# One core, attention beside an SSM: a rewrite with a played-out order, three-bank exps, tables made once, a bound from |q| and transposed reciprocals

## The chip, the cores and the metric

The kernel runs on one core of a Trainium2 chip. The metric is device microseconds of that core, lower is better.

Engine names as in the profile: PE (TensorE matmuls), PEld (its weight loads), DVE (VectorE), ACT (ScalarE), POOL (GpSimd), SP (the queue that issues most DMAs). A trailing q, as in ACTq, is an engine's instruction sequencer. "Pass" in this document means 512 columns streamed through PE once, by one matmul or by several that run side by side in different parts of the array.

## The reference

Two independent layers, concatenated on the last axis.

```python
# A: a diagonal complex SSM, L = 2048, D = P = 640
dt = exp(log_dt); Lam_bar = exp(dt * Lam)
B_bar = ((Lam_bar - 1) / Lam)[:, None] * Bmat
Bu = einsum("bld,pd->blp", x, B_bar)
h_t = Lam_bar * h_{t-1} + Bu_t                  # 2048 steps
y = 2 * einsum("blp,dp->bld", h, Cmat).real + x * Dskip

# B: attention, 32 query heads of 20, one shared key/value head, S = 2048
q = (x @ wq) in 32 heads; k = x @ wk; v = x @ wv
p = softmax(q k^T * 20**-0.5)                   # 32 x 2048 x 2048
out = (p v, heads joined) @ wo
```

Inputs and output are bf16. The large object is the 134 million softmax weights: 2048 tiles of 128 keys by 512 queries, each of which must go once through ACT's exp.

## The kernel before

Attention is walked in 512 iterations of 4 tiles. Scores need only 21 contraction rows (20 plus one that carries the softmax bound), so four heads sit in PE's four row groups. An iteration scores two tiles into two PSUM banks (SCA), two more into two others (SCB), takes an exp of each pair, and adds the four tiles, multiplied by the values (the PV matmuls), to a PV bank, four column groups at once.

```python
def plan_scores(self, it, half):
    T = self.SCA if half == 0 else self.SCB
    for jj in range(2):
        j = 2 * half + jj
        P.pe(lambda e: e.matmul(T[:, 512*jj:512*jj+512],
             lhsT=P.KT[32*j:32*j+21, 128*kc:128*kc+128],
             rhs=P.QT[32*j:32*j+21, gg, q0:q0+512], tile_position=(32*j, 0), ...), ...)
def plan_exp(self, it, half):                   # 1024 columns each
    P.act(lambda e: e.activation(ptv, T[:, :], ACT.Exp, scale=self.alpha), ...)
def plan_pv(self, it):
    for j in range(4):
        P.pe(lambda e: e.matmul(pvt[32*j:32*j+32, :], lhsT=P.VP[:, kc, 0:32],
             rhs=P.PT[:, buf, j, :], tile_position=(0, 32*j), ...), ...)
```

Everything else is background, laid into these iterations by fixed rates (4 PE steps an iteration, then 3 DVE steps, and so on):

```python
self.BG_PE_PER_IT, self.BG_DVE_PER_IT, self.OUTPROJ_PER_IT = 4, 3, 6
...
def qt_block_ops(self, gg, tb, ps, bkey):
    # q: 5 passes over xbT with wq4; then the bound: 5 more over |x| with wm4 (from |wq| and max|k|)
    ...
def ssm_tables_ops(self, tb):
    # for each of 4 token blocks: 30 DVE steps and 10 Sin activations on ACT
    ...
def norm_tasks(self, gi):
    # sums of 4 heads -> 4 partitions x 512, reciprocal there, broadcast by a matmul
    d2 = ... e.reciprocal(rden, den_ps)         # 4 x 512
```

## Time and profile before

| | before |
|---|---|
| time, median of 4 runs | 1250.8 us (1246.3 to 1251.1) |
| first exp starts, last exp ends, span (timeline) | 73.6, 1226.2, 1249.5 us |
| exps, smallest start-to-start | 1024, 0.903 us |
| mean granted PE clock | 0.705 |

From the page of the kernel before: span, busy time by engine, the slices of PE, ACT and granted clock (in tenths), and the chain of waits.

```profile
span 1249.5 us, 12936 instructions
...
PE 987.0 (79%) x5371; PEld 261.0 (21%) x5442; DVE 513.5 (41%) x772; ACT 1016.6 (81%) x1089; POOL 18.0 (1%) x24
...
PE   2678888887788786888885788888858788889886
...
ACT  4067898989888898888988888898978888898882
...
PEclk9777997986666766776656766766656777675777
...
ACT 51%; PE 36%; DVE 9%; issue 2%; SPq 1%; DMA 0%; ACTq 0%; DVEq 0%
```

ACT and PE are both busy for about 80% of the time and neither is full. The chain passes from one to the other. The clock row holds tenths, but the records behind it know only 0.5 and 1.0; a 7 is a slice that changed in between.

From the page's groups (busy us, mean ns of one, idle before and what ended it), and from the view of waits (us in total, times, longest):

```profile
L780 ACT ACTIVATE PT<-SCA 128x1024 bf16<-128x1024 f32 x512 | 529.6, 1034 | 151.0 <-PE SCB L767 122.1
L780 ACT ACTIVATE PT<-SCB 128x1024 bf16<-128x1024 f32 x512 | 530.6, 1036 | 0.0
...
L817 DVE RECIPROCAL rdenb<-PVB 4x512 bf16<-4x512 f32 x16 | 53.5, 3346 | 37.2 <-PE PVB L812 37.2
```

```profile
ACT PT L780 <- PE SCB L767: 122.1, 90, 2.3
...
ACT PT L780 <- PE SCA L767: 27.3, 53, 4.2
```

ACT waits for scores 143 times for 149 us in all. The timeline shows what such a wait looks like, here at half clock, with background work (line 631) between the score groups:

```profile
320.51 0.62 PE L792 MATMUL PVA<-PT,VP 128*32 128x512 bf16 x4
320.82 1.02 ACT L780 ACTIVATE PT<-SCB 128x1024 bf16<-128x1024 f32 x1
...
321.46 1.49 PE L631 MATMUL M<-xaT,BTre 128*128 128x512 bf16 x3 [0.33 <-issue]
...
322.88 0.61 PE L767 MATMUL SCA<-QT,KT 21*128 21x512 bf16 x2
...
323.55 1.02 ACT L780 ACTIVATE PT<-SCA 128x1024 bf16<-128x1024 f32 x1 [1.72 <-PE SCB L767]
```

Between the exp that starts at 320.82 and the next, at 323.55, PE put background passes before the scores, and ACT stood for 1.72 us. In undisturbed stretches exps start 0.90 to 0.92 us apart.

### The profile page before, as it was taken

How to read it: one execution, taken by the hardware profiler on the slowest of the kernel's cores; microseconds unless marked ns; L12 is line 12 of the kernel's file. 1: busy time of each engine (PE TensorE's matmuls, PEld its weight loads, DVE VectorE, ACT ScalarE, POOL GpSimd, SP SyncE). 2: the span in 40 equal slices, each digit the busy share in tenths (PEclk: the TensorE clock that was granted, in tenths of full speed). 3: DMA queues.
4: the chain of work that ended last, by engine and by line, in shares of the span. 5: the costliest groups of instructions: out<-in, count | busy, mean ns of one | idle time of the engine just before them, and what ended most of it. 6: DMA issues, size and time to landing. Idle time of an engine off the chain costs nothing.

```text
span 1249.5 us, 12936 instructions
## 1 busy us (share of the span) xinstructions
PE 987.0 (79%) x5371; PEld 261.0 (21%) x5442; DVE 513.5 (41%) x772; ACT 1016.6 (81%) x1089; POOL 18.0 (1%) x24
## 2 busy tenths in 40 slices
PE   2678888887788786888885788888858788889886
PEld 1212222221112211221111222211112222111222
DVE  0522211226542278225773242266951213675222
ACT  4067898989888898888988888898978888898882
POOL 5000000000000000000000000000000000000000
PEclk9777997986666766776656766766656777675777
DMA  9700000000000000000000000000000000000000
GB/s 180 142 6 1 1 1 1 1 1 1 1 1 11 11 1 1 11 12 1 1 1 5 17 1 11 11 1 1 1 6 6 17 12 6 1 1 1 11 12 21
DMA packets 44179, 16.29 MB, mean 13 GB/s; under 512 B 38744, under 2 KB 44120, under 8 KB 44120
## 3 DMA queue, kind: packets, MB, share of 16 engines
q1 hardware_dynamic: 44120, 15.46, 5.4%
q8 instruction: 42, 0.69, 0.2%
q14 instruction: 17, 0.14, 0.0%
HBM read 1.69 MB, written 5.24 MB: 6 GB/s over the span
## 4 chain that ended last, share of the span: by engine, by line
ACT 51%; PE 36%; DVE 9%; issue 2%; SPq 1%; DMA 0%; ACTq 0%; DVEq 0%
ACT PT L780 48%; PE SCA L767 5%; PE SCB L767 5%; PE M L631 4%; PE M L516 3%; PE PVA L792 3%; PE PVB L792 3%; PE M L837 3%; PE M L715 2%; DVE rdenb L817 2%; ACT tab L613 2%; PE M L522 1%; PE M L719 1%; PE M L840 1%; SPq L381 1%
## 5 line engine op out<-in xcount | busy, mean ns | idle before, releaser
L780 ACT ACTIVATE PT<-SCA 128x1024 bf16<-128x1024 f32 x512 | 529.6, 1034 | 151.0 <-PE SCB L767 122.1
L780 ACT ACTIVATE PT<-SCB 128x1024 bf16<-128x1024 f32 x512 | 530.6, 1036 | 0.0
L767 PE MATMUL SCB<-QT,KT 21*128 21x512 bf16 x1024 | 262.3, 509 | 118.1 <-ACT PT L780 107.9
L767 PE MATMUL SCA<-QT,KT 21*128 21x512 bf16 x1024 | 267.1, 500 | 74.9 <-ACT PT L780 73.3
L792 PE MATMUL PVA<-PT,VP 128*32 128x512 bf16 x1024 | 134.0, 514 | 0.0
L792 PE MATMUL PVB<-PT,VP 128*32 128x512 bf16 x1024 | 133.7, 511 | 0.3 <-ACT PT L780 0.3
L767 PEld LDWEIGHTS SCA<-QT,KT 21*128 21x128 bf16 x1024 | 50.9, 95 | 288.4 <-ACT PT L780 241.4
L767 PEld LDWEIGHTS SCB<-QT,KT 21*128 21x128 bf16 x1024 | 50.8, 95 | 279.4 <-ACT PT L780 277.2
L526 DVE CAST QT<-M 128x512 bf16<-128x512 f32 x26 | 18.0, 692 | 125.8 <-PE M L522 125.8
L817 DVE RECIPROCAL rdenb<-PVB 4x512 bf16<-4x512 f32 x16 | 53.5, 3346 | 37.2 <-PE PVB L812 37.2
L817 DVE RECIPROCAL rdenb<-PVA 4x512 bf16<-4x512 f32 x16 | 53.5, 3344 | 31.9 <-PE PVA L812 31.8
L742 DVE CAST ystage<-M 128x512 bf16<-128x512 f32 x16 | 11.0, 687 | 115.2 <-PE M L715 115.2
L846 DVE CAST ostage<-M 128x512 bf16<-128x512 f32 x16 | 11.1, 691 | 110.5 <-PE M L837 68.4
L837 PE MATMUL M<-WO,OT 128*128 128x512 bf16 x114 | 50.2, 505 | 2.3 <-DVE ostage L846 2.3
L811 DVE CAST pvsb<-PVB 128x512 bf16<-128x512 f32 x16 | 11.1, 691 | 95.9 <-PE PVB L792 95.9
L792 PEld LDWEIGHTS PVA<-PT,VP 128*32 128x32 bf16 x1024 | 27.2, 97 | 90.2 <-issue 88.9
L792 PEld LDWEIGHTS PVB<-PT,VP 128*32 128x32 bf16 x1024 | 27.3, 97 | 89.4 <-issue 87.5
L516 PE MATMUL M<-xbT,wq 128*128 128x512 bf16 x117 | 44.0, 490 | 1.5 <-issue 1.5
L631 PE MATMUL M<-xaT,BTre 128*128 128x512 bf16 x80 | 39.6, 598 | 6.7 <-issue 5.7
L522 PE MATMUL M<-xabsT,wm 128*128 128x512 bf16 x124 | 40.3, 428 | 2.3 <-issue 2.3
L811 DVE CAST pvsb<-PVA 128x512 bf16<-128x512 f32 x16 | 11.0, 690 | 67.7 <-PE PVA L792 67.7
L715 PE MATMUL M<-CimT,W 128*128 128x512 bf16 x80 | 38.3, 478 | 0.0
(162 smaller groups left out, 797.4 us busy)
## 6 DMA issues: line engine op xcount, KB each, us to landing
out_dram<-ostage SPq DMA_DIRECT2D x16, 160.0 KB, 1.8
out_dram<-ystage SPq DMA_DIRECT2D x16, 160.0 KB, 1.8
wq_raw<-in_B_wq_dram SPq DMA_DIRECT2D x1, 800.0 KB, 5.9
WO<-in_B_wo_dram SPq DMA_DIRECT2D x4, 200.0 KB
xbT<-in_B_x_dram SPq DMA_TRANSPOSE x5, 5.3
xaT<-in_A_x_dram SPq DMA_TRANSPOSE x5, 5.5
BTre<-in_A_B_re_dram SPq DMA_TRANSPOSE x5, 2.9
BTim<-in_A_B_im_dram SPq DMA_TRANSPOSE x5, 2.9
```

The costliest lines, as they stand in the source:

```text
L516: pe_ops.append(dict(fn=lambda e, c=c, st=(n == 1): e.matmul(ps, lhsT=P.wq4[:, c, gg, :], rhs=P.xbT[:, c, 512 * tb:512 * tb + 512], start= ...
L522: pe_ops.append(dict(fn=lambda e, c=c, sp=(n == 2 * NC): e.matmul(ps, lhsT=P.wm4[:, c, gg, :], rhs=P.xabsT[:, c, 512 * tb:512 * tb + 512], ...
L526: dve_ops = [dict(fn=lambda e: e.tensor_copy(P.QT[:, gg, 512 * tb:512 * tb + 512], ps), reads=[bkey], writes=[f"QT{gg}_{tb}", "qtdone"])]
L613: act_ops.append(dict(fn=lambda e, c=c, cs=cs, src=src: e.activation(P.tab[:, buf, cs, c, :], P.ang_f[:, c, src, :], ACT.Sin, scale=TWO_PI ...
L631: pe_ops.append(dict(fn=lambda e, mt=mt, BT=BT, cd=cd: e.matmul(mt[:, :], lhsT=BT[:, cd, 128 * c:128 * c + 128], rhs=P.xaT[:, cd, 512 * tb ...
L715: pe_ops.append(dict(fn=lambda e, lhs=lhs, CT=CT, c=c, st=(nmm6 == 1), sp=(nmm6 == total6): e.matmul(o6, lhsT=lhs, rhs=CT[:, c, 0:512], st ...
L767: P.pe(lambda e, jj=jj, j=j: e.matmul(T[:, 512 * jj:512 * jj + 512], lhsT=P.KT[32 * j:32 * j + 21, 128 * kc:128 * kc + 128], rhs=P.QT[32 * ...
L780: P.act(lambda e: e.activation(ptv, T[:, :], ACT.Exp, scale=self.alpha), reads=[keys[0], keys[1]], writes=[f"PT{buf}_{half}"])
L792: P.pe(lambda e, j=j: e.matmul(pvt[32 * j:32 * j + 32, :], lhsT=P.VP[:, kc, 0:32], rhs=P.PT[:, buf, j, :], start=(kc == 0), stop=(kc == se ...
L811: d1 = dict(eng="dve", fn=lambda e: e.tensor_copy(pvsb, pvt[:, :]), reads=[pvkey], writes=[pvsb_key])
L817: return e.reciprocal(rden, den_ps)
L837: pe_ops.append(dict(fn=lambda e, lhs=lhs, rh=rh, st=st, sp=sp: e.matmul(P.M6[:, 0:512], lhsT=lhs, rhs=rh[:, 0:512], start=st, stop=sp), r ...
```

## The change

The intent is to keep ACT fed. The program is written as steps with estimated durations; an event simulation at build time plays them out and fixes each engine's order. Besides:

1. Score groups and exps span three banks (3 + 3 of the 8): 683 exps of 1536 columns, three row groups of PE at once.
2. Sin tables are made once for 512 tokens; the SSM state is rotated between blocks. That leaves ACT's loop with exps alone.
3. The softmax bound comes from |q| (one small matmul per block) and goes into QT's extra row by small DMAs, in place of 5 full passes per q block.
4. Denominators are transposed first: reciprocals of 128x16 instead of 4x512, spread by POOL and brought back by PE.
5. SSM products are 1024 wide, and inputs arrive in 512-row pieces.

The diff replaces nearly the whole file; its core:

```diff
-class Planner:                         # order as the program text gives it, fixed rates
+class Schedule:                        # event simulation; picks by readiness and priority
+    OUT = {"pe": 200.0, "act": 130.0, "dve": 110.0, "pool": 150.0, "dma": 60.0}
+    def mmt(n, k=1):
+        return n / 2.3 * 1.0 + 8.0 * k     # ns of one pass
...
+    CHUNKS = (3, 3)
+    MISC = 1                            # one bank for all background work, one for PV
+    def fill(self, op, i):
+        for x in range(n):              # n = 3
+            op.fns.append(self.mm(t[:, 512*x:512*x+512], p.KT[32*j:32*j+21, 128*kc:128*kc+128],
+                                  p.QT[32*j:32*j+21, qb % 2, gg, :], True, True, tile_position=(32*j, 0)))
+        ex = self.act(lambda e: e.activation(dst, t[:, 0:512*n], ACT.Exp, scale=1.0 / UNIT), ...)
...
-            pe_ops.append(... e.matmul(ps, lhsT=P.wm4[:, c, gg, :], rhs=P.xabsT[...] ...)   # x5 per q block
+    def row_task(self, qb, half, bank):
+        fns = [self.mm(bank.tensor[0:32, ...], p.Mm[:, gg, :], p.aq[:, gg % 4, :], ...) for gg in ggs]
+        fns = [lambda e: e.dma_start(p.QT[32*j+20:32*j+21, slot, gg, :], p.brow[8*j+gg:8*j+gg+1, rs, :])
+               for gg in ggs for j in range(4)]
+        self.row_op[(qb, half)] = self.dma(fns, ..., "sp" if qb else "act", ...)
...
-                return e.reciprocal(rden, den_ps)                              # 4 x 512
+            return e.reciprocal(p.rdT[:, slot, :], bank.cols(0, 16))           # 128 x 16
+        x = self.pool(lambda e: e.tensor_copy(p.rdX[:, slot, :, :], spread), ...)
```

## The prediction

> **What bounds it now.** The span is 1249.5 us. The chain of waits gives ACT 51%, PE 36%, DVE 9%; exp alone is 48%. The page's groups show 1024 exps of 128x1024, mean 1035 ns. In the timeline undisturbed exps start 0.90-0.92 us apart: a floor of 925 us. They run from 73.6 to 1226.2 us, 1153 us. The other 228 us are lost: 34 us (estimate) to Sin tables and ACT table switches, about 190 us to exps waiting for scores. The lead-in is 73.6 us, the tail 23 us.
>
> The loss is PE running slow in lumps. The granted clock is only ever 1.0 or 0.5, mean 0.705, so about 60% of the time is slow: the two states of the Trainium skill (TensorE: Matmul & The Clock Gate, Part 1). A 512-column pass takes 427 or 215 ns; a change between score, PV and full-array matmuls costs 0.1 us more, into full-array ones up to 0.5. An iteration (two exps) without background matmuls takes 1.83 us even at half clock; with four it takes 3.7 us at half clock, 1.98 at full. Background work in slow stretches is the loss.
>
> **What changes.**
> 1. Exp over three banks: 683 instead of 1024. The Trainium skill (ScalarE: Activation LUTs, What ACT_TABLE_LOAD costs) gives 186 + 0.833 N ns; the trace agrees in length (1035) but shows more overlap, so spacing is 0.833 N + 50. Estimate: 1.33 us spacing, 1.465 us length, floor 908 us. Only 17 us saved.
> 2. Three scores in one pass: 683 passes instead of 1024. Abs-q bound: 160 passes become 32. Background in the main loop 842 -> about 730 passes. PE at half clock: 1.44 us per exp on average against 1.33; before, per iteration, 2.27 against 1.81.
> 3. Sin tables once, before the loop: 34 us off ACT. DVE falls from 513 to about 320 us (no 3.35 us reciprocals), but is off the critical path; only the last normalisation gains, 3 us, partly given back by the new GpSimd copy.
> 4. Lead-in: no |wq| products (10 us of DVE), no wait for all loads; but the tables, 32 small bound DMAs and their issues on ACT come around the first exp. First exp at 43 us (35-52).
> 5. The played-out order assumes about 230 ns per pass, the fast clock. In it some 150 of 683 intervals still carry 3 to 5 background passes; at half clock such an interval needs 2.3-2.9 us, so lumps still stall ACT.
>
> **Sum (estimate).** Charging each interval of the order the larger of 1.33 us and its passes at measured cost gives 1.68 us at half clock, 1.36 at full; the same arithmetic on the old order gives 2.42 and 1.84, where 2.19 was measured (without tables), so 60% slow. That gives 1.55 us, 1060 us; slack in the double buffer takes off perhaps 20. Lead-in 43, tail 20: about 1105 us. Gains: lead-in 30, tables 34, PE stalls 60-80.
>
> Chances: faster by over 2% 0.95, within 2% 0.03, slower 0.02.
>
> **What would show it.** Exp count 683, mean 1.46 us, spacing 1.33; first exp near 43; mean exp spacing 1.45-1.6; clock 0.6-0.75; exps released by PE scores inside background lumps; no table loads after the first exp; PE chain share 25-40%.
>
> **What would make it wrong.** A clock that stays at half because spread work never triggers full speed (1165), or turns out fast (1025); PE, in order, held by the GpSimd copy, by the single PV bank's eviction or by the misc bank; ACT held by issuing row DMAs.

## The result, and the profile after

The changed kernel takes 1113.9 us (median of 4 runs, 1109.5 to 1117.4) against 1250.8 us. The ratio is 0.8915, 95% interval 0.8883 to 0.8946: faster. A ratio is the mean time of one kernel's fast runs over that of the other's of the same rounds, so it is not quite the ratio of the medians quoted.

The page after, the same rows as before:

```profile
span 1108.9 us, 12552 instructions
...
PE 855.2 (77%) x5435; PEld 236.9 (21%) x5504; DVE 310.5 (28%) x504; ACT 947.0 (85%) x701; POOL 36.8 (3%) x54
...
PE   3548887788778788888778878887778778877776
...
ACT  2268989999998989999999899899998989989991
...
PEclk9755567668677867667767777668865676577656
...
ACT 52%; PE 34%; DVE 6%; issue 5%; ACTq 2%; DMA 1%; POOL 0%; POOLq 0%; DVEq 0%
```

The exp group and the waits of ACT, from the groups and the view of waits:

```profile
L798 ACT ACTIVATE PR<-SC 128x1536 bf16<-128x1536 f32 (+1 forms) x683 | 933.1, 1487 | 96.9 <-PE SC L484 86.7
```

```profile
ACT PR L798 <- PE SC L484: 86.7, 120, 1.5
...
ACT PR L798 <- issue: 9.1, 1, 9.1
```

ACT is fuller, but PE still holds a third of the chain and the clock is no higher than before (0.689 against 0.705). The lead-in, from the timeline around the first exp:

```profile
42.72 10.34 ACTq L732 DMA_DIRECT2D QT<-brow  x16
...
53.11 1.06 ACT L992 ACTIVATE tab<-fr 128x1024 bf16<-128x1024 f32 x1 [10.18 <-DVE prod L495]
54.18 1.28 ACT L798 ACT_TABLE_LOAD   x1
56.30 1.45 ACT L798 ACTIVATE PR<-SC 128x1536 bf16<-128x1536 f32 x1 [0.83 <-PE SC L484]
56.30 10.51 ACTq L732 DMA_DIRECT2D QT<-brow  x16
...
66.86 5.48 ACT L798 ACTIVATE PR<-SC 128x1536 bf16<-128x1536 f32 x4 [9.12 <-issue]
```

ACT's queue spends 10.3 us issuing 16 small DMAs before the last Sin can run, and 10.5 us issuing 16 more after the first exp. The releaser that the profile names for the Sin (DVE prod) is an inference; the row above it shows what the queue was doing.

The two profiled runs, split at the first exp's start and the last exp's end. The floor is the number of exps times their smallest spacing, 1024 x 0.903 and 683 x 1.330; the table time of the kernel before is what experiment b_tab1 below took off its main loop.

| us | before | after | difference |
|---|---|---|---|
| lead-in | 73.6 | 56.3 | -17.3 |
| main loop | 1152.6 | 1029.2 | -123.4 |
| – floor of the exps | 924.7 | 908.4 | -16.3 |
| – Sin tables and table switches | 34.6 | 0 | -34.6 |
| – ACT's queue issuing DMAs | 0 | 9.1 | +9.1 |
| – the rest, ACT not fed | 193.3 | 111.7 | -81.6 |
| tail | 23.3 | 23.4 | 0 |
| span | 1249.5 | 1108.9 | -140.6 |

"The rest" is more than the waits view adds up to (149 and 87 us), since exps that follow without a wait overlap: an exp of 1.45 us is spaced 1.33 us from the next, and a wait first eats that overlap.

### The profile page after: what moved, and what is told of

Same layout as the page of the kernel before. It is cut to its first block, busy times and chain, and to the rows that moved or that the text cites. A ratio compares the mean times of both kernels' runs of the same rounds, so it can differ in the third digit from the quotient of the medians.

```text
span 1108.9 us, 12552 instructions
## 1 busy us (share of the span) xinstructions
PE 855.2 (77%) x5435; PEld 236.9 (21%) x5504; DVE 310.5 (28%) x504; ACT 947.0 (85%) x701; POOL 36.8 (3%) x54
## 4 chain that ended last, share of the span: by engine, by line
ACT 52%; PE 34%; DVE 6%; issue 5%; ACTq 2%; DMA 1%; POOL 0%; POOLq 0%; DVEq 0%
ACT PR L798 52%; PE MB L484 23%; PE SC L484 10%; ACTq L732 2%; DVE prod L491 2%; DVE g L1079 1%; DVE sc L960 0%; POOL rdX L880 0%; DVE sc L495 0%; DVE QT L700 0%; DVE u L491 0%; DVE ost L923 0%; DMA vec<-in_A_log_dt_dram 0%; DMA QT<-brow 0%; DVE pvsb L859 0%
## 5 line engine op out<-in xcount | busy, mean ns | idle before, releaser
L798 ACT ACTIVATE PR<-SC 128x1536 bf16<-128x1536 f32 (+1 forms) x683 | 933.1, 1487 | 96.9 <-PE SC L484 86.7
L484 PE MATMUL SC<-QT,KT 21*128 21x512 bf16 x2048 | 351.1, 509 | 180.1 <-ACT PR L798 169.0
L484 PE MATMUL MB<-PR,VP 128*32 128x512 bf16 x2048 | 270.8, 516 | 1.3 <-ACT PR L798 1.0
L484 PEld LDWEIGHTS SC<-QT,KT 21*128 21x128 bf16 x2048 | 69.5, 95 | 462.6 <-ACT PR L798 400.7
L491 DVE TENSOR_TENSOR prod<-MB,Z 128x1024 bf16<-128x1024 f32 x40 | 49.0, 1224 | 219.5 <-PE MB L484 206.3
L484 PEld LDWEIGHTS MB<-PR,VP 128*32 128x32 bf16 x2048 | 55.7, 98 | 174.9 <-issue 170.8
L484 PE MATMUL MB<-xaT,BT 128*128 128x512 bf16 x170 | 72.5, 538 | 9.5 <-issue 7.5
L484 PE MATMUL MB<-CT,W 128*128 128x128 bf16 (+1 forms) x304 | 68.3, 367 | 5.0 <-issue 4.6
L484 PE MATMUL MB<-WO,OT 128*128 128x128 bf16 (+1 forms) x247 | 56.3, 381 | 9.5 <-DVE ost L923 2.4
L484 PE MATMUL MB<-xbT,wq 128*128 128x512 bf16 x127 | 50.7, 508 | 6.8 <-issue 3.3
```

The costliest lines, as they stand in the source:

```text
L484: return lambda e: e.matmul(out, lhsT=lhsT, rhs=rhs, start=start, stop=stop, **kw)
L491: return lambda e: e.tensor_tensor(out, a, b, op)
L798: ex = self.act(lambda e: e.activation(dst, t[:, 0:512 * n], ACT.Exp, scale=1.0 / UNIT), 0.833 * 512 * n + 93, deps=[op], reads=[b.key for ...
```

## The experiments

Twelve kernels ran. All but one are single (one time and a profile), so differences under about 10 us are not to be trusted by the total alone. The kernel before gave 1252.5 us beside the first four, 1246.2 beside the next four, and a median of 1250.9 beside the last four. "Main loop" is from the first exp's start to the last exp's end, "full" the share of the clock windows in it that stood at 1.0.

| run | edit | us | main loop | full |
|---|---|---|---|---|
| (before) | | 1250.8 | 1152.6 | 0.38 |
| (after) | | 1113.9 | 1029.2 | 0.35 |
| rows4 | 4 bound DMAs, not 16 | 1097.8 | 1022.6 | 0.36 |
| dup1 | every score twice | 1205.4 | 1122.4 | 0.38 |
| pad | scores repeated in light intervals | 1159.0 | 1072.5 | 0.42 |
| coldorder | order for half clock | 1209.3 | 1100.9 | 0.08 |
| order20 | order for 256 ns a pass | 1112.9 | 1029.5 | 0.31 |
| k32 | scores with 32 rows | 1089.2 | 1007.6 | 0.45 |
| padfull | full-array dummies in light intervals | 1053.1 | 966.0 | 0.83 |
| b_tab1 | before, tables once | 1216.1 | 1118.0 | 0.40 |
| a_22 | groups of two banks | 1314.0 | 1231.1 | 0.11 |
| b_nobound | before, no bound passes | 1252.6 | 1167.8 | 0.29 |
| b_recip | before, copy for reciprocal | 1243.3 | 1148.9 | 0.38 |
| best | padfull + k32 + rows4 + order20 | 1007.4 | 933.2 | 0.92 |

My theory at first: PE feeds ACT too slowly in stretches of half clock, because lumps of background work stand between score groups. Rivals: the lumps do not matter, only the sum of PE's work does; or the clock answers to the work, so that taking work away takes clock away. A separate question was the lead-in.

### 1. The bound DMAs on ACT's queue (rows4)

```diff
-        fns = [lambda e, j=j, gg=gg: e.dma_start(p.QT[32*j+20:32*j+21, slot, gg, :], p.brow[8*j+gg:8*j+gg+1, rs, :])
-               for gg in ggs for j in range(4)]
+        fns = [lambda e, j=j: e.dma_start(p.QT[32*j+20:32*j+21, slot, g0:g0+4, :], p.brow[8*j+g0:8*j+g0+4, rs, :])
+               for j in range(4)]
```

> The changed kernel, but the bound rows of a half block go to QT in 4 DMAs of 4 rows instead of 16 DMAs of 1 row (same bytes). Theory (ScalarE's queue issues them one by one, 0.65 us each: 10.3 us before the last Sin and the first exp, 9.1 us after the first exp): the first exp starts 6 to 8 us earlier, near 49 us, the wait after the first exp falls from 9.1 to about 2.5 us, total 1094 to 1102 us. Rival (tables on VectorE and the DMAs' landing hold the first exp anyway): under 4 us gained in all.

Measured: 1097.8 us, 16 us less than the median of the changed kernel. The timeline has the queue busy for 3.3 and 2.4 us, and the first exp at 49.7 instead of 56.3 us:

```profile
42.97 3.29 ACTq L733 DMA_DIRECT2D QT<-brow  x4
...
49.73 1.45 ACT L799 ACTIVATE PR<-SC 128x1536 bf16<-128x1536 f32 x1 [1.06 <-PE SC L484]
49.74 2.42 ACTq L733 DMA_DIRECT2D QT<-brow  x4
...
52.20 12.19 ACT L799 ACTIVATE PR<-SC 128x1536 bf16<-128x1536 f32 x9 [1.02 <-DVE prod L495]
```

The theory holds. What costs is the count of DMAs that ACT must issue (0.65 us each), not their bytes: the same bytes in a quarter of the DMAs took a quarter to a third of the time. The Trainium skill (Trainium Kernel Development and Optimization, Key Constraints) says that issuing from several engines "only saves the sequencer's issue time"; here the issue time had been put on the one engine that could not spare it.

### 2. Does the clock follow the load? (dup1, pad)

Reading the clock records window by window (they come in multiples of 3.41 us, as the Trainium skill says in TensorE: Matmul & The Clock Gate, Part 1), I first thought that a window at full clock stays full when passes fill half of it. So more passes should raise the clock, even useless ones.

```diff
+        op.fns = op.fns * 2                 # dup1: each group of three scores issued twice
```

```diff
+                    need = self.PAD_TO - passes + carry            # pad: only in intervals with few passes
+                    k = min(self.PAD_MOST, max(0, round(need)))
+                    fill.fns = fill.fns * (k + 1)
```

> The changed kernel with every score matmul issued twice (same result, 683 more 512-column passes of PE). Clock theory (the two traces: a 3.41 us window at full clock stays full when passes fill over half of it, one at half clock turns full at 0.75 to 0.85): windows without background rise from 0.56 to 0.88 busy at half clock and turn full, but at full clock fill only 0.44 and fall back; share of full clock rises from 0.35 to 0.5-0.6 of the main loop, total within 25 us of 1111 although PE has 24% more passes. Rival (the clock does not follow the load; more passes are more work): at unchanged clock shares the arithmetic of the prediction gives about 1.84 us per exp, total over 1250 us.

> The changed kernel with score matmuls repeated only in intervals of PE's order that have little other work, up to about 3.3 passes per exp (563 more passes, same result). Clock theory: windows at full clock never fall under half busy, so the clock stays full, mean 0.93 or more in the main loop; score waits shrink, exp spacing mean 1.36 to 1.42 us, total 1015 to 1050 us: more work, less time. Rival (more work only): total over 1200 us at an unchanged clock.

Both missed: 1205.4 and 1159.0 us, the full share only 0.38 and 0.42 against 0.35. Repeating scores bought little clock and cost PE time. Granted clock by slices, dup1 and then pad:

```profile
PEclk9755665667777968657867878667666778677657
```

```profile
PEclk9756666558767977568878877677767787577656
```

But the rival's sum did not come out either (it said over 1250 and over 1200). The traces told why: in these runs windows at half clock that passes filled often stayed at half. In dup1 matmuls filled over 95% of 171 such windows, and 126 of these were followed by half clock again. A score pass drives 3 x 21 of the 128 rows; a background pass drives all. Fitted to the traces then at hand, a window's next state followed the passes weighted by kind: background most, PV next, scores least.

### 3. The weighted load (k32, padfull)

So the second theory: what counts is passes weighted by the part of the 128x128 array that they use. Two edits separate it from "more work": k32 adds no pass at all, padfull adds passes of the heaviest kind.

```diff
-    p.KT[32*j:32*j+21, ...], p.QT[32*j:32*j+21, ...]      # k32: rows 21 to 31 are zeros in both operands
+    p.KT[32*j:32*j+32, ...], p.QT[32*j:32*j+32, ...]
```

```diff
+                    need = self.PAD_TO - load + carry              # padfull: load weighted, a score group counts 0.49
+                    k = min(self.PAD_MOST, max(0, round(need)))
+                    lhs = p.wq4[:, 0, 0:4, :].rearrange("p h d -> p (h d)")
+                    fill.fns = [self.mm(bank.ap, lhs, p.xbT[:, 0, 0:512], True, True)] * k + fill.fns
```

The dummy writes a bank that the score group behind it overwrites, so the result is unchanged.

> The changed kernel with score matmuls that use all 32 rows of their row group instead of 21 (rows 21 to 31 of both operands hold zeros; same result, same passes, same columns). Weighted-clock theory (fitted to the runs so far: a window at full clock stays full when passes, each weighted by the part of the 128x128 array that it uses, fill 0.37 of it; at half clock 0.70 to 0.75; the mean over the main loop is 0.327 of full rate): the mean load rises to about 0.36, the share of full clock in the main loop from 0.35 to 0.42-0.60, total 1060 to 1098 us. Rival (the clock counts passes, or whole row groups, or does not see zero rows): clock share 0.35 +- 0.03, total within 8 us of 1111.

> The changed kernel with dummy full-array matmuls (128x128 weights, 512 columns, into the bank that the next score group overwrites) in intervals of PE's order with little other work, up to a weighted load of 2.6 full passes per exp. Same result. Weighted-clock theory: full clock for over 0.8 of the main loop, exp spacing mean 1.36 to 1.44 us, total 1020 to 1065 us although PE does more. Rival (extra work only costs, as repeated scores did: 1159 and 1205): total over 1150 us, full clock for under 0.55.

Both held, each in one run. k32: 1089.2 us, full share 0.45, for an edit that changes one number and no instruction count. padfull: 1053.1 us, full share 0.83, with several hundred more full-array matmuls. Granted clock by slices, k32 and then padfull, to be read against the row of the changed kernel above:

```profile
PEclk9755667667778887768868888777867777677657
```

```profile
PEclk9855999989989869889989999699999999989996
```

In padfull the waits of ACT for scores fell from 86.7 to 32.6 us:

```profile
ACT PR L824 <- PE SC L510: 32.6, 60, 2.2
```

With all traces in hand the rule can be counted. For every 3.41 us window of the main loops of these fourteen traces I summed the streaming time of each matmul (columns over the clock granted), weighted it by its active rows and columns over 128 x 128, and expressed it as a share of what the array could do at full clock. Then I looked at the clock of the next window:

| weighted load of the window | windows at half clock, of them next at full | windows at full clock, of them next at full |
|---|---|---|
| under 0.275 | 1392, 8 | 342, 0 |
| 0.275 to 0.325 | 417, 44 | 135, 18 |
| 0.325 to 0.375 | 522, 191 | 218, 103 |
| 0.375 and more | 354, 348 | 1046, 1029 |

The same load decides in both states, near 0.35 of the full-rate array. At half clock PE can reach at most 0.5, so it climbs out only in dense stretches. The mean load in the main loop was 0.29 before, 0.31 after, 0.35 in k32, 0.43 in padfull, 0.46 in best: the kernels before and after sit just under the point where the clock stays up. The mean alone does not decide: dup1 and pad had 0.36, coldorder 0.30, with full shares of 0.38, 0.42 and 0.08. What counts is how the load falls on the windows. The middle rows are not sharp; windows are cut by my alignment, some matmul records can be missing, and I fitted no second parameter.

One rival is that the clock follows PE's busy time, whatever the matmuls. A second count of the same traces (its windows differ from the table's by a few) speaks against it. Matmuls filled over 95% of 1015 windows at half clock. With a weighted load of 0.375 or more, 336 of 340 were followed by full clock; with less, only 60 of 675. But the weight by area is not the exact rule: between 0.325 and 0.375, 54 of 342 of these filled windows rose, against 132 of 180 that were 80 to 95% filled.

### 4. The order (order20, coldorder)

```diff
-        return n / 2.3 * 1.0 + 8.0 * k
+        return n / 2.0 + 8.0 * k            # order20
+        return n / 1.2 + 8.0 * k            # coldorder: half clock
```

> The changed kernel, its order played out with 427 ns + 8 per 512-column pass (half clock) instead of 223 + 8. Theory (the order was made for the fast clock, lumps of 3 to 5 background passes between two score groups stall exps at half clock): smaller lumps, ScalarE idle in the main loop falls from 97 us to 40-70, total 1060 to 1090 us. Rival A (PE has too little time at half clock whatever the order, 1.44 us of work per 1.33 us): within 15 us of 1111. Rival B (evenly spread work never fills a window, so the clock falls): clock under 0.62 and total above 1120 us.

> The changed kernel, its order played out with 256 + 8 ns per pass instead of 223 + 8, which takes the intervals with 6 passes from 93 to 3 without starving the block rows. Lump theory: the arithmetic of the prediction gives 15 to 24 ns less per exp, main loop 10 to 16 us shorter, total 1093 to 1103 us. Rival (lump size does not matter, only the sum of PE's work): within 6 us of 1111.

order20 removed nearly all of the large lumps (intervals with 6 passes: 3 instead of 93) and gained nothing: 1112.9 us, main loop 1029.5 against 1029.2. The full share fell from 0.35 to 0.31 (mean clock 0.669; the four runs of the changed kernel had 0.681 to 0.690). The arithmetic of the prediction with the measured clock shares gives 1.569 us per exp for the changed kernel (0.646 x 1.682 + 0.354 x 1.364) and 1.565 for order20 (0.688 x 1.667 + 0.312 x 1.340), so by this arithmetic the two effects cancel; with one run it is argued, not shown. The rival's forecast (within 6 us of 1111) held, and my theory of lumps falls as a reason by itself.

coldorder is a poor test of what it was meant for. The order-maker, told that PE is slow, starved the bound rows of the next blocks behind output work, and the loop stood still ten times for 4 to 17 us from one exp to the next. Its first exp came at 80.3 us, 24 us later than in the changed kernel, which is part of the 1209.3 us:

```profile
DVE brow L496 <- PE MB L484: 126.5, 6, 35.5
...
ACT PR L798 <- PE MB L484: 100.0, 10, 15.7
```

On the clock side, the full share was 0.08 with work spread evenly, and both figures of rival B came out (clock 0.561, over 1120 us). The stalls lower the load too, so how much of the low clock is the even spread stays open.

### 5. What single parts are worth (b_tab1, b_recip, b_nobound, a_22)

Three parts tried alone on the kernel before, and one undone in the changed kernel.

```diff
-                if c == self.NC - 2 and tb + 1 < self.NQB:     # b_tab1: tables of block 0 used for all (SSM half wrong)
+                if False:
```

> The kernel before with the Sin tables of the first token block only, used for all four (SSM half wrong on purpose; attention half right). Prediction: tables and table switches cost ScalarE 34 us, of which nearly all shows, since exps are the chain: total 1208 to 1222 us. Rival (they fall into waits for scores and hide): total over 1235 us.

1216.1 us; the main loop is 34.6 us shorter. As predicted.

```diff
-                return e.reciprocal(rden, den_ps)              # b_recip (attention half wrong)
+                return e.tensor_copy(rden, den_ps)
```

> The kernel before with the reciprocal of the softmax denominator (3.35 us each, 32 times) replaced by a copy of the same shape (attention half wrong on purpose). Prediction: VectorE is off the chain but for the last block, so 85 us less of its work gives 2 to 8 us: total 1240 to 1250 us. Rival (slow reciprocals hold up background work and PV banks in the loop): total under 1232 us.

1243.3 us against 1250.9, at the upper end of what was expected and close to the noise of a single look. Within the trace the main loop is 3.7 us shorter and the tail 3.0 us (20.3 against 23.3). So 32 reciprocals of 3.35 us were indeed nearly free, except for the last.

```diff
-        for c in range(NC):                                    # b_nobound: no wm4 passes
+        for c in range(0):
```

> The kernel before without the matmuls of the softmax bound (130 passes fewer in the main loop, 30 before it; scores are small enough that the result should still be right). Prediction's arithmetic at 60% half clock: 28 us less in the main loop, a few us in the lead-in, total 1210 to 1225 us. Rival (weighted clock: those were full-array passes that kept the clock up; with them the full-clock share falls and gives the gain back): full-clock share of the main loop falls from 0.38 to under 0.33, total 1232 us or more.

1252.6 us: nothing gained, although PE has 160 passes fewer (by the order 120 in the loop and 40 before it; the expectation said 130 and 30). The first exp came 14 us earlier (59.4), the main loop became 15 us longer, and the full share fell from 0.38 to 0.29. The result was still right. The rival holds (it said under 0.33 and 1232 us or more): full-array passes were carrying the clock, and removing them gave the time back.

```profile
PEclk9766675656656766666567776755675776766657
```

```diff
-    CHUNKS = (3, 3)
+    CHUNKS = (2, 2)                                            # a_22
```

> The changed kernel with score groups and exps over two banks instead of three (the new order-making and all else kept). Theory (what three banks buy is passes of PE, three row groups used at once, not ScalarE time): PE 2.22 passes per 0.90 us exp, so the arithmetic of the prediction, scaled to what it gave for the three-bank kernel, gives a main loop of 1110 to 1150 us instead of 1029, total 1185 to 1225 us. Rival (it only buys the 17 us of exp overhead): 1120 to 1140 us.

1314.0 us, slower than the kernel before and far above both expectations. Part of it is long waits of the kind seen in coldorder, which I had not foreseen: six, 72 us in all, behind background matmuls. Even without those it would be some 1242 us, 128 us above the changed kernel. The exps' floor explains 16 us of that. The rest goes with the clock: full share 0.11, mean load 0.26.

```profile
ACT PR L798 <- PE SC L484: 163.1, 205, 1.1
...
ACT PR L798 <- PE MB L484: 72.0, 6, 17.0
...
PEclk9655555655557665555556856555755755555556
```

So in this order-maker the rest of the rewrite, without three banks and with the 72 us set aside, is about where the kernel before is (1242 and 1251 us): the gain needs the three banks. That three banks alone would bring it is not shown; they were not tried in the kernel before. How much is passes and how much is clock can't be told apart from this run, since each feeds the other.

### 6. All that helped (best)

> The changed kernel with four of the edits together: dummy full-array matmuls in light intervals (weighted load up to 2.7 passes per exp), 32-row score matmuls, bound rows in 4 DMAs, order played out with 256 ns per pass. Weighted-clock theory plus the arithmetic of the prediction at over 0.85 of full clock (1.34 to 1.38 us per exp): first exp near 50 us, main loop 925 to 950 us, tail 24, total 1000 to 1028 us. Rival (the gains overlap, padding and 32 rows both only buy clock): total 1035 us or more.

1007.4 us, median of 4 runs (1005.3 to 1013.9), correct, and as expected (1000 to 1028). The ratio to the kernel before is 0.8064, 95% interval 0.8029 to 0.8099. It beats both kernels.

```profile
span 1006.2 us, 13243 instructions
...
ACT  1389999999999999999999999999999999999991
...
PEclk9879999988799989999999999989989999999998
...
ACT 79%; PE 11%; DVE 5%; issue 3%; POOL 1%; ACTq 1%; DMA 0%; POOLq 0%; DVEq 0%
...
L825 ACT ACTIVATE PR<-SC 128x1536 bf16<-128x1536 f32 (+1 forms) x683 | 920.7, 1624 | 15.0 <-PE SC L510 13.3
```

Its main loop is 933 us, 25 us above the 908 us floor of the exps. order20's smoother order was included because at full clock lumps are all that is left to stall ACT; it was not run without, so its share in this version is open.

## Why the prediction was right, point by point

The time was right: 1105 us predicted, 1113.9 measured. Not all of its terms were, and luck had a part: an error in the lead-in and one in the main loop nearly cancelled, and the clock, taken as given, happened to stay near its old share.

- *"683 instead of 1024 ... 1.33 us spacing, 1.465 us length, floor 908 us. Only 17 us saved."* Right: 683, 1.330 us, 908.4 us, 16.3 us. The mean length was 1487 ns, as exps that follow closely are recorded longer (1451 when alone); in best it is 1624 at the same spacing. Spacing is what to read.
- *"Sin tables once, before the loop: 34 us off ACT."* Right: 34.6 us (b_tab1).
- *"DVE falls from 513 to about 320 us ... but is off the critical path; only the last normalisation gains, 3 us, partly given back."* Right: 310.5 us. b_recip shows 3.0 us in the tail and little in the loop. In the changed kernel the tail as a whole is as long as before (23.4 and 23.3 us).
- *"First exp at 43 us (35-52)."* Wrong: 56.3 us. The step that failed is the size of the DMA issues. The prediction named "32 small bound DMAs and their issues on ACT", but its sum shows no term for them (its list of what would make it wrong has "ACT held by issuing row DMAs"). They are 0.65 us each: rows4 took 6.6 us off the lead-in, and the main loop too was 6.6 us shorter, where its second batch lies. Of the predicted gain of 30 us, 17 came. rows4 explains 6.6 of the 13 us that are missing, and the 3.3 us which its queue still spends on the first batch may be more of them; the rest is not accounted for.
- *"so 60% slow"* and *"clock 0.6-0.75"*: right in size, 64.5% and 0.689. *"That gives 1.55 us ... slack in the double buffer takes off perhaps 20"*: 1.507 us measured, so a main loop of 1029 us where 1040 was predicted; the 9 us of DMA issues are inside it. The shortfall in the lead-in and this surplus nearly cancelled, which is luck.
- *"Background work in slow stretches is the loss"* and *"lumps still stall ACT"*: right as a description of where ACT waits, not as a cause by itself. order20 took the lumps away and gained nothing; padfull left them in, added work, and gained 61 us.
- *"Abs-q bound: 160 passes become 32"* was booked as a gain in PE's time. Alone on the kernel before it gained nothing (b_nobound). The prediction took the clock as given, 60% slow whatever the work. k32, padfull and b_nobound show that the work sets it. That the changed kernel came out at nearly the old share (0.35 full against 0.38) was not derived.
- Under what would make it wrong, *"a clock that stays at half because spread work never triggers full speed"* was the right worry. It did not come true for the change (0.35 full against 0.38), it did for coldorder and a_22 (0.08 and 0.11).

Where the 82 us less of unfed ACT come from is shown only in part: without three-bank groups the gain is gone (a_22). What the event simulation itself contributes, against fixed rates with the same parts, was not isolated; no run puts the old order around the new parts. That stays open.

## What to carry to other kernels

When the granted clock hovers between its two states, count the load of PE per window, weighted by the part of the array that each matmul uses, before taking work off PE: removing full-array passes can give all of its gain back. If ACT bounds the loop and PE has spare time, widen small-row matmuls to whole row groups and fill light intervals with full-array dummies; that was worth 25 and 61 us here, in one run each. Count the DMAs that the bounding engine must issue, not their bytes.

## What the Trainium skill lacked or had wrong

- TensorE: Matmul & The Clock Gate, Part 1 says that the gate follows how busy PE has been and that idle windows throttle it; the practical rule is to avoid idle gaps of over about 3 us. The page also tells of clock lost to frequent short idles between groups. The two states and the 3.41 us windows agree with the records here. Lacking: the load counts by array use. A PE that streams all the time can stay at half clock: of 1015 half-clock windows that matmuls filled to over 95%, 619 were followed by half clock. And in 576 of 589 windows after which full clock was lost, PE had no idle gap as long as 1 us (modelled ends). In 342 of 342 windows with a weighted load under 0.275 of full rate the full clock was lost, in 1029 of 1046 with 0.375 or more it was kept. Active rows count even when they hold zeros: 32 rows for 21 raised the full share from 0.35 to 0.45.
- The same page (Why this matters for your kernels) advises to keep PE busy without gaps, and does not say with which matmuls (of transposes alone Part 4 says that they do not count the same way). Here repeats of the scores left the full share at 0.38 and 0.42; full-array dummies took it to 0.83.
- ScalarE: Activation LUTs, What ACT_TABLE_LOAD costs: back-to-back activations are said to overlap by about 93 ns. Here exps of 1024 columns (1023 ns after an idle gap of 0.3 us or more) start 903 ns apart, and of 1536 columns (1451 ns) 1330 ns apart: an overlap of about 120 ns. The length in the record grows when they follow closely (mean 1624 ns in best at the same spacing), so it is no measure of cost.
- DMA: Bandwidth & Descriptors, Issuing engines are not separate DMA queues: the time to initiate a DMA is called "usually small relative to the DMA itself". Here ACT's queue took 0.65 us for each of 16 DMAs of 1 KB (10.3 us in all, where one lands a median 3.1 us after its issue), and 0.6 to 0.8 us for each of 4 DMAs of 4 KB. For one such DMA the page is right (0.65 of 3.1 us); sixteen in a row kept ACT from its other work for 10.3 us.
